# Half of the modulation weights in one transfer, freer PSUM banks and a new order in a transformer block with a gated spatial MLP

## The chip, the cores and the metric
One core of one Trainium2 chip runs the whole program. The metric is device microseconds (us) of one execution. Engines are called by their names and by the letters of the profile: TensorE is PE (its weight loads PEld), VectorE is DVE, ScalarE is ACT, GpSimd is POOL, SyncE is SP. SP and ACT issue the DMA transfers of this kernel.

## What is computed
An adaptive-layer-norm block on 2048 tokens of width 448, all tensors bf16. A vector `c` of 448 numbers gives six modulation vectors; then sliding-window attention (16 heads of 28, window 256), then a gated MLP whose gate mixes tokens with a 2048 x 2048 matrix:

```python
mod = (silu(c) @ w_mod).reshape(1, 6, 1, 448)      # w_mod: 448 x 2688
sa, ca, ga, sb, cb, gb = mod
h = layernorm(x) * (1 + ca) + sa
x = x + ga * attention(h, wqkv, wo)                 # 0 <= q - k < 256
h = layernorm(x) * (1 + cb) + sb
z = gelu(h @ w_in)                                  # 448 -> 1792
z1, z2 = z[:, :896], layernorm(z[:, 896:])
x = x + gb * ((z1 * (w_sp @ z2 + b_sp)) @ w_out)    # w_sp: 2048 x 2048
```

## The kernel before
**Tiles.** The 2048 tokens are 16 tiles of 128. The first half of the block runs over six blocks of tiles (1, 1, 2, 4, 4, 4). The width of 448 is cut into four chunks of 128 rows that start at rows 0, 128, 192 and 320 (`CH`); chunks 1 and 2 overlap in rows 192 to 255, and one of the two overlapping halves is zeroed or left out.

**Operations and their order.** The program is a list of some 1700 operations (`P.op`, with helpers `pe`, `dve`, `pool` and `load`), numbered in the order in which the code makes them. The string `ORDER` (line 177) lists these numbers in the order in which they are issued; `75/3` takes the fourth of the PSUM banks that the operation may use, `65.2` the third of its engine choices. `schedule` (line 81) reads the string and `emit` (line 115) turns it into one in-order stream for each engine, with a semaphore wait where an operation needs another engine's result, a DMA or a buffer that is still in use. An operation that waits holds up all that stands behind it on its engine; nothing else sets the order.

**Names used below.** `wmodA01`, `wmodA3`, `wmodAR0`, `wmodAR1`: loads of the part of w_mod for sa and ca (lines 496 to 499). `wqk03`, `wqkM`, `wqkR0`, `wqkR1`: loads of the query and key weights in raw form (lines 505 to 509). `x0`, `x0b`, `x1` to `x4`: tokens of tiles 0, 1, 2-3, 4-7, 8-11 and 12-15. `silu` (line 556): silu of c in column form, made from the row by `c_cols`. `modA` (line 585): 16 small matmul operations, eight for chunks 0 and 1 and eight (with an h) for chunks 3 and 2, all into one PSUM bank; `modAe` (line 588) evicts them to `modT`, the scale and shift. `l1_ts` (bn_stats, line 603), `ag`, `ve`, `rs`, `nm`: layer-norm statistics of tile t; `xn` the normalized tile (lines 624 and 625). `tr`: transposes of xn on TensorE for the first three blocks (line 674); `hT` evicts them with the modulation (lines 687 and 692). The last three blocks are transposed by DMA (`hx`, line 709) and modulated in place (`hm`, line 701). `wqkf` and `wqkr` spread the raw weights into padded form (lines 725 to 727). `qk<block>_<group>` are the query and key projections (lines 776 and following; for tile 0 partly from the raw weights, on 32 columns at a time), `qke` their evictions to `QKT` (lines 810 and 813), `v` and `ve` the values (lines 822 and 825).

**Attention.** For query tile j, `S<j>_<u>` writes scores of one key tile to two pairs of PSUM banks, `E<j>_<u>` takes the exponential on ScalarE (128 x 1024 elements, line 912, 90 of them, tiles `PT`), `M<j>_<u>` zeroes what the mask excludes on POOL (line 918), `PV` multiplies with the values, and `oq`, `rec`, `nrm`, `oT`, `wo`, `x1` normalize, transpose and project (lines 944 to 964). Projections of later blocks, and the first of the MLP, stand between the scores on TensorE. `gateB` (line 967) and four `woutg` multiplications (line 968) fold the last gate into w_out.

**The rest.** After the last scores come z2 and z1 of the MLP, the 448 matmuls with w_sp (`G`, whose stationary operand is z2), and the output projection, all on TensorE, with evictions on ScalarE and DVE.

The modulation's loads before, with the c row first on ScalarE's queue, are the lines that the diff below removes. The rows of chunk 2 that chunk 1 doesn't have (256 to 319) are loaded as two pieces of 64 rows, `wmodAR0` for sa into partitions 0 to 63 and `wmodAR1` for ca into partitions 64 to 127, and `c_cols` makes a fifth column of silu(c) so that each half of the chunk meets its own half of the column.

Of the kernel before, what the change touches and what calls it, by code (L numbers as in the profile page):

```python
# [181 lines left out]
142 155 14 252 156 248 157 20 159 160 161 188 189 499/0,0 162 163/0 164 165 501/4 166 168/1 173/2 174 167 21 250 249 254 143/3 251 144 175 16 169 170
171 176 145 146 147 113/0 114 115 116 117 191.1/4 196/0 253 148/3 149 255 256 172 150 151 152 337 190.1/2 195 333 257 258 262/3 177 261.1/1 500/1,1
504/0 192/3 193 194.1 22 197 11 178/1 179 180 181 182.1 123/4 124 516/0,1 125 126 127.1 520/2 228/0 229 230 231 232 15 497/3 208/0 209 210 211 331 18
19 498 218/2 219 517/6 212 266 220 221 222 523/1,0 526/8 223/1 259.1/0 224 198/2 199 225 502 200 524/10 201 202.1 226 505 506/0 503 507/0 203/3 204
205 206 265 260.1/2 207 508 338 335 233/2 234 235 236 237 332 227 521 537/0,1 541/7 518 213/3 334 214 519/0 509.1/1 336 339 263 215 216 217.1 340 525
522 527 528/0 243/1 244 245 246 264 267 270 268 269 341 345/3 538/8 238/3 239 240 544/1,0 344.1/4 420 241 539 418 247 271/1 326/0 327 281/2 282 548/6
328 349 329 330.1 272 273 283 545/1 551/1,0 343.1/0 284 285.1 342/2 242 552/5 306/3 307 308 309 291/0 310.1 274 554/4 292 293 294 419 348 565/0,1
566/10 347 529 530.1/0 549 276/3 277 275.1 278 311/2 312 313 314 279 569/0 570 295.1 510/0 416 417 315 286/0 287 572/0,1 573/9 288 289 531/1 301/1
576/3 302 303 304 280.1 579/0,2 580/2 290.1 540/0 582/8 546 547 555 550 542 543 553 305.1 421 296/1 297 298 299 593/1,0 556/0 557 532/0 533 567 534  # L190
535 577 300.1 511/1 512 513 514 594/1 600/2,1 414 536 597/4 574 575/0 568 571 346 351.1 558.1/1 583 353.1 578 581 598 559/2 350.1 515 560/1 561 562
352.1 604/7 607/1,0 584/0 563 564 601/6 602 585 932 379/0 415 380 381 382 383.1 929 364/1 365 931 610/10 595 621/2,0 964 605 366 367 586.1/1 368.1
608/9 384/0 385 930 386 387 422 388.1 587/2 934 622/2 623 625/3 628/1,2 632/5 369/1 370 371 372 373.1 606/0 629/7 603 423 424 428.1/1 611 596 426.1/2
609 599 635/0,2 612/0 636/9 588/1 589 590 591 592 432 359/0 360 649/0,1 427.1/3 638/6 653/4 321/1 322 966 323 324 613 361 362 656/1,2 650/1 935 325.1
399/1 400 401 402 425.1/0 633 363.1 967 946/0 947 948 949 660/10 614.1/1 950 962 951 952 953 663/2,0 626 403.1 316/1 317 318 319 657/0 661 630 954
637/0 627 639 624 960 615/1 664/8 677/2,1 654 320.1 634 631 666/9 640/0 641 651 354/1 355 356 357 358.1 658 659/0 652 642.1/1 431 965 961 963 968 969
678/5 667 684/0,2 681/7 688/6 685/1 689 643/2 655 662 665 668/0 682 374/1 375 376 377 378.1 691/1,2 694/9 669 644/0 645 646 1419 647 648 430 692/0 429
433.1 389/1 390 391 392 937 705/2,0 709/10 404/0 405 406 970 407 706/3 393.1 409/1 410 411 679 712/1,0 412 686 985 436.1 408.1 616/0 617 618 413.1
435.1 619 933 434.1 716/4 457/1 458 670.1/0 620 717 719/0,2 973/1 459 460 461.1 695/0 683 713/8 971/2 722/2 710 707 693 687 690 680 1421 733/1,2 936
696/0 697 720/9 734/7 737/1 394/1 395 396 938 397 398.1 452/0 453 454 455 740/1,0 467/1 735 671/2 468 469 470 456.1 672/0 673 674 675 983 744/6  # L200
747/0,2 471.1 447/1 698.1/1 448 449 941 738 676 739/0 714 972 987 450 451.1 741/0 742 699/1 750/5 761/1,2 736 751 743 745 748/1 762/7 746 765/6 749
752/0 975/0 437/1 438 439 440 441.1 768/1,0 772/5 942 977/2 974 753 754/1 763 715/0 708 711 769/10 770 700/1 701 702 703 704 775/0,2 984 978 755/0 721
718 723 773 724/0 725 462/1 463 464 465 776/1 778/3 466.1 789/0,1 793/4 989 442/0 976 726.1/0 443 444 940 445 990 446.1 790/2 482/1 483 484 485
796/2,1 797/8 771/0 486.1 727/1 766 981.1 777 774 779 764 767 988 780/0 800/0 979.1 487/1 939 803/2,0 986 806/7 945 991 804/3 488 489 490 472/0 473
474 475 980 817/1,0 821/9 801 491.1 756/1 781 757 758 759 992 476.1 782.1/1 728/0 729 791 730 731 818/5 798 760 824/0,2 828/6 783/0 784/1 785 786 819
825/1 732 1006 802/0 787 799 788 1423 822 1008 794 993 831/2,1 829 477/1 834/0 832/10 478 479 826 792 1010 480 845/0,1 998/1 795 846/4 481.1 807 805
808/0 955/1 809 849/8 1420 943 944 957 810.1/0 852/0,2 853/3 999 827/0 833 823 835 820 830 836/0 859/1,0 956 982.1 1075/0 1077 847 1076 856/10 1059/2
1000/0 1060 811/2 958 860/9 812/3 813 814 815 959 857 1422 1061 816 1012 862/2 873/1,0 874/5 1080/1 1079 1078 850 1081 1065/3 1082 877/6 1063 1062
1064 1067.1 1007 1013 854 855/0 848 996/2 1066 1009 880/0,1 837 851 997 994.1/1 838/0 863 1083 1011 1014 1015 884/3 885 1091/3 1092 1097/2 881/7 1096
839/0 1095 1001 1093 1094 1098.1 1099 861 858 864/0 865 887/1,0 888/0 1016 1107/1 1108 1109 492/3 493 494 495 890/1 1112/2 1111 866/0 1023/0 496 1110  # L210
867/1 901/0,1 902/9 1113 1115 868/0 1021/2 1114 869 870 871 908/0,2 872 905/10 882 1031 840/1 841 842 843 909/4 995 1004.1 1002.1 1302/7 1303 1304
1311/2 1314/6 1312 1313 912/8 915/2,0 1424 1317 1316 913 878 1003 1315 916/2 1005 844 1338/3 1339 1340 1167/2 1173 1169 1029 1030 875 1172 1168
1017.1/1 1171 1022 1170 1318 876/0 889 891 879 883 886 903 1319 1306/6 1307 1019/2 1305 1174/3 1123/3 1125 1126/2 1032 1127 892/0 893 917/0 1128 914
910 911 904 894.1/0 1176 1308 1129 1033 906 895/0 1124 918/7 919 907 1139/0 1429 1142 1141 1024 1143 1131 1342/0 1343 1144 1310 1341 1140 1329/6 1331
# [987 lines left out]
```

## Time and profile before
| | us |
|---|---|
| median of 3 runs | 271.27 |
| lowest, highest | 271.03, 271.34 |
| the profiled execution | 271.53 |
| its span, first to last instruction | 269.8 |

| engine | busy us | share of the span |
|---|---|---|
| PE | 258.7 | 96% |
| DVE | 168.2 | 62% |
| ACT | 133.2 | 49% |
| POOL | 104.1 | 39% |

The profile's page gives each engine's busy time, a picture of the span in 40 slices, the DMA queues, the chain of work that ended last (followed back from the last instruction to what released it) and groups of instructions. Its views can be narrowed to a stretch of the span; all times in them are us from the span's start. "Idle before" with a name behind an arrow says how long the engine sat before an instruction, and what ended that. A matmul's end is modelled, and matmuls overlap, so busy times of PE are an upper figure. The granted clock is the share of TensorE's full clock that was given.

### The profile page before, as it was taken

Reading aid. Unit: us, or ns where it says so; the run is one execution under the profiler, and the core shown is the slowest. Engines: PE = TensorE matmul, PEld = TensorE weight load, DVE = VectorE, ACT = ScalarE, POOL = GpSimd, SP = SyncE. Lnnn points to the kernel's source line nnn. Section 1 sums busy time; section 2 is a strip of 40 time slices with the busy share of each in tenths; the row PEclk is TensorE's granted clock in tenths of the full one; section 3 lists DMA queues with packets and bytes.
Section 4 is the critical chain, followed back from the end, with each engine's and each line's share of the span. In section 5 each row is a group of like instructions: output and inputs, shape, how many; then the busy total and the mean of one; then the engine's idle time right before and its main releaser. Section 6 shows DMA issues by size and latency. Waiting matters only on the chain.

```text
span 269.8 us, 7133 instructions
## 1 busy us (share of the span) xinstructions
PE 258.7 (96%) x3067; PEld 128.4 (48%) x3090; DVE 168.2 (62%) x390; ACT 133.2 (49%) x183; POOL 104.1 (39%) x162
## 2 busy tenths in 40 slices
PE   6799999999999799999999999999999999999995
PEld 2567444564545444544444444444444444444453
DVE  4499888887898899579968920731511534335343
ACT  4599899999999989986786200000000000100000
POOL 3566489889968848771732120000000000000000
PEclk9799999999999999999999999999999999999999
DMA  6945262298359434679599890000000000000103
GB/s 221 348 149 84 23 146 88 52 153 164 73 80 231 44 71 81 117 90 158 126 205 161 184 185 1 2 0 0 0 2 0 17 0 17 2 16 18 53 34 119
DMA packets 61052, 23.72 MB, mean 88 GB/s; under 512 B 49886, under 2 KB 60893, under 8 KB 61021
## 3 DMA queue, kind: packets, MB, share of 16 engines
q1 hardware_dynamic: 60715, 22.92, 42.2%
q8 instruction: 24, 0.39, 0.6%
q10 hardware_dynamic: 306, 0.35, 0.4%
q14 instruction: 7, 0.06, 0.1%
HBM read 9.36 MB, written 1.84 MB: 41 GB/s over the span
## 4 chain that ended last, share of the span: by engine, by line
PE 78%; ACT 8%; DVE 5%; DMA 4%; POOL 2%; issue 1%; ACTq 1%; SPq 0%; DVEq 0%
PE ps L457 73%; ACT PT L912 8%; PE ps L454 5%; DMA wmod_sb<-in_w_mod_dram 2%; DMA hT<-xn 1%; DVE st_all L603 1%; DVE w_out_sb L968 1%; POOL xn L624 1%; POOL PT L918 1%; DVE QKT L813 1%; PE ps L776 1%; DVE hT L701 1%; POOL rs_all L611 0%; DVE xn L625 0%; DVE hT L692 0%
## 5 line engine op out<-in xcount | busy, mean ns | idle before, releaser
L912 ACT ACTIVATE PT<-ps 128x1024 bf16<-128x1024 f32 x90 | 84.7, 1054 | 3.0 <-PE ps L457 2.5
L1041 ACT ACTIVATE z1T<-ps 128x512 bf16<-128x512 f32 x28 | 15.0, 602 | 82.5 <-PE ps L457 82.4
L1110 DVE TENSOR_TENSOR tmpg<-ps,bsp_bc 128x512 bf16<-128x512 f32 x28 | 19.1, 689 | 56.1 <-PE ps L457 55.7
L457 PE MATMUL ps<-QKT,z 128*128 128x512 bf16 x220 | 50.7, 379 | 0.2
L918 POOL TENSOR_SCALAR_AFFINE_SELECT PT<-PT 128x512 f32<-128x512 f32 x60 | 36.6, 635 | 4.8 <-ACT PT L912 4.6
L457 PEld LDWEIGHTS ps<-QKT,z 128*128 128x128 bf16 x224 | 21.9, 98 | 26.2 <-ACT z1T L1041 0.3
L611 POOL TENSOR_TENSOR rs_all<-ve_all,neghalf 128x1 f32<-128x1 f32 (+2 forms) x27 | 18.5, 686 | 32.6 <-DVE ve_all L610 32.2
L457 PE MATMUL ps<-w_spD,z 128*128 128x512 bf16 x109 | 26.0, 379 | 0.2
L457 PE MATMUL ps<-w_spC,z 128*128 128x512 bf16 x108 | 25.1, 379 | 0.2
L457 PE MATMUL ps<-hT,w_in_sb 128*128 128x512 bf16 (+1 forms) x95 | 23.5, 380 | 0.3 <-issue 0.2
L457 PE MATMUL ps<-w_in_sb,hT 128*128 128x448 bf16 (+1 forms) x102 | 22.8, 353 | 0.3 <-POOL PT L918 0.3
L457 PE MATMUL ps<-w_out_sb,z1T 128*128 128x448 bf16 (+2 forms) x119 | 22.8, 341 | 0.0
L457 PE MATMUL ps<-hT,WQK 128*128 128x512 bf16 (+2 forms) x118 | 20.7, 304 | 1.1 <-ACT QKT L810 0.4
L624 POOL TENSOR_SCALAR xn<-x_sb,rs_all,nm_all 128x512 bf16<-128x512 bf16 x25 | 19.7, 793 | 4.5 <-DVE nm_all L641 3.9
L603 DVE BATCH_NORM_STATS2 st_all<-z2raw 128x6 f32<-128x448 bf16 x32 | 18.8, 609 | 1.5 <-ACT z2raw L1018 1.0
L457 PE MATMUL ps<-QKT 28*128 28x128 bf16 x720 | 18.3, 217 | 1.5 <-ACT PT L912 1.1
L603 DVE BATCH_NORM_STATS2 st_all<-x_sb 128x6 f32<-128x448 bf16 x32 | 19.4, 616 | 0.3
L1132 DVE TENSOR_TENSOR fin<-ps,x_sb 128x448 bf16<-128x448 f32 (+2 forms) x17 | 9.9, 595 | 13.8 <-PE ps L457 13.7
L813 DVE CAST QKT<-ps 128x512 bf16<-128x512 f32 (+1 forms) x26 | 16.9, 655 | 2.1 <-PE ps L454 1.0
L457 PEld LDWEIGHTS ps<-QKT 28*128 28x128 bf16 x720 | 10.4, 92 | 16.4 <-ACT PT L912 13.4
L457 PEld LDWEIGHTS ps<-w_spD,z 128*128 128x128 bf16 x112 | 11.0, 98 | 13.0
L457 PEld LDWEIGHTS ps<-w_spC,z 128*128 128x128 bf16 x112 | 10.9, 98 | 13.1
(94 smaller groups left out, 325.9 us busy)
## 6 DMA issues: line engine op xcount, KB each, us to landing
wmod_sb<-in_w_mod_dram SPq DMA_DIRECT2D x8, 224.0 KB, 5.5
w_in_sb<-in_B_w_in_dram SPq DMA_DIRECT2D x8, 224.0 KB, 3.9
out_dram<-fin SPq DMA_DIRECT2D x16, 112.0 KB, 1.7
x_sb<-in_A_x_dram SPq DMA_DIRECT2D x3, 448.0 KB, 6.1
bsp_bc<-in_B_b_sp_dram SPq DMA_DIRECT2D x1, 512.0 KB, 5.3
wqk_raw<-in_A_wqkv_dram SPq DMA_DIRECT2D x1, 452.0 KB, 5.7
wmod_sb<-in_w_mod_dram SPq DMA_DIRECT2D x1, 448.0 KB, 4.7
wv_sb<-in_A_wqkv_dram SPq DMA_DIRECT2D x2, 224.0 KB, 5.9
```

The costliest lines, as they stand in the source:

```text
L454: last = e.matmul(out_[32 * j:32 * j + 32], lhsT=lhsT[:, 32 * j:32 * j + 32], rhs=rhs, start=st, stop=sp, tile_position=(0, 32 * j), **kw)
L457: return e.matmul(out_, lhsT=lhsT, rhs=rhs, start=st, stop=sp, **kw)
L603: st = [dve("%sst%d" % (name, i), prio, dve_ns(D), lambda e, i=i, s_=s_: e.bn_stats(st_all[:, slot, t, i, :], s_()), deps, tens) for i, s_ ...
L611: r = pool(name + "rs", prio, 420 + 148 * n, lambda e: e.tensor_tensor(rs_all[:, slot, t0:t1], ve_all[:, slot, t0:t1], neghalf[:, t0:t1], ...
L624: return e.tensor_scalar(dst, src, rs_all[:, slot, t:t + 1], nm_all[:, slot, t:t + 1], ALU.mult, ALU.add)
L701: return e.tensor_scalar(hT[:, c_, cols], hT[:, c_, cols], modT[:, base_col + 4 + c_:base_col + 5 + c_], modT[:, base_col + c_:base_col + ...
L813: return e.tensor_copy(QKT[:, g, cols], ps[:, ten.slot, 0:w])
L912: e_op = P.op("E%d_%d" % (j, ui), pr, [("act", 925, lambda e, e_in=e_in, e_out=e_out: e.activation(e_out(), e_in(), ACT.Exp, scale=SCALE)) ...
L918: ready = pool("M%d_%d" % (j, ui), pr - 50, pool_ns(512), lambda e, pt=pt, pat=pat, cm=cm, cmp=cmp: e.affine_select(out=pt32(pt.slot), in_ ...
L1041: g = P.op("z1g%d_%d" % (tb, ft), pr - 19, [("act", act_ns(512), lambda e: e.activation(z1T[:, ft, tb * 512:(tb + 1) * 512], ps[:, ten.slo ...
L1110: a = dve("ga%d_%d" % (tb, ft), pr, dve_ns(512), lambda e, tb=tb, ten=ten, tg=tg: e.tensor_tensor(tmpg[:, tg.slot, :], ps[:, ten.slot, :], ...
L1132: fs.append(dve("fin%s%d" % (nm, t), pr, dve_ns(c1 - c0), lambda e, t=t, ten=ten, ft_=ft_, c0=c0, c1=c1: e.tensor_tensor(fin[:, ft_.slot, ...
```

## The change
**Loads.** `wmodA3`, `wmodAR0` and `wmodAR1` (224, 56 and 56 KB) go; `wmodA23` comes, rows 192 to 447 in one transfer of 448 KB, on ScalarE's queue behind the c row as `wmodA3` was. Rows 192 to 255 are then in SBUF twice; the column of silu(c) for chunk 2 has zeros there. So `c_cols` has four matmuls and not five, one of the three copies of the c row on DVE goes (`cz2`), and `silu` works on four columns.

**Banks.** The single PSUM banks of `c_cols`, of `modA` and of the transposes of tile 1 (block 1) could be one of four, and can now be any of the eight.

```diff
-             load("wmodA3", -98, lambda e: e.dma_start(wmod_sb[:, 3, 0:2 * D], w_mod[320:448, 0:2 * D]), 128 * 2 * D * 2, order=[t_c], eng="act")]
-    t_wmAR = [load("wmodAR%d" % v, -98, lambda e, v=v: e.dma_start(wmod_sb[64 * v:64 * v + 64, 2, 0:D], w_mod[256:320, v * D:(v + 1) * D]), 64 * D * 2, eng="act")
-              for v in range(2)]
...
+             load("wmodA23", -98, lambda e: e.dma_start(wmod_sb[:, 2:4, 0:2 * D], w_mod[192:448, 0:2 * D].rearrange("(c p) n -> p c n", p=128)),
+                  256 * 2 * D * 2, order=[t_c], eng="act")]
...
-    tc_ten = Ten(B_D)
+    tc_ten = Ten(B_ALL)
...
-        for k, a in enumerate((0, 128, 256, 448, 320)):
-            last = mm(e, ps[:, tc_ten.slot, k:k + 1], crz[0:1, a:a + 128], one[0:1, 0:1], True, True)
+        for k in range(4):
+            last = mm(e, ps[:, tc_ten.slot, k:k + 1], crz[0:1, 128 * k:128 * k + 128], one[0:1, 0:1], True, True)
...
-            dve("cz1", -62, 180, lambda e: e.tensor_copy(crz[0:1, 320:384], crow[0:1, 256:320]), [t_c]),
-            dve("cz2", -62, 180, lambda e: e.tensor_copy(crz[0:1, 448:576], crow[0:1, 320:448]), [t_c])]
+            dve("cz1", -62, 180, lambda e: e.tensor_copy(crz[0:1, 320:512], crow[0:1, 256:448]), [t_c])]
...
-    mA_ten = Ten(B_D, guard=True)
+    mA_ten = Ten(B_ALL, guard=True)
...
-                for kc, sc in (((0, 0), (1, 1)), ((3, 3), (2, 4 if i == 0 else 2)))[h]:
-                    a = CH[mc] + (0 if kc == 2 else i * D)
+                for kc, sc in (((0, 0), (1, 1)), ((3, 3), (2, 2)))[h]:
+                    a = CH[mc] + i * D
...
-            ten = Ten(B_ALL if b == 0 else B_D, guard=True)
+            ten = Ten(B_ALL if b < 2 else B_D, guard=True)
```

**Order.** `ORDER` is new from end to end. Read with the names, each engine's stream changes most up to the first exponentials:

```
SP before    x0 wmodA01 wqk03 x0b wqkR0 wqkR1 x1 wqkM wv1 x2 woq2 x3 wmodG1 x4 wv0 ...
SP after     x0 wmodA01 wqk03 x0b wqkR0 x1 wqkR1 wqkM wv1 x2 wv0 wmodG0 wmodG1 woq2 x3 ...
ACT before   c wmodA3 wmodAR0 wmodAR1 silu0 silu exp0 hT0_3 wqkf1_3 hT0_0 wqkr0_k hT0_1
             wqkr0_q wqkf1_M qke0_5 wqkr1_q qke0_0 qke0_1 qke0_4 hT1_1 (6 qke) E0_0
             (6 qke) E0_1 hT2_1 E1_1 qke2_3 E1_0 (2 qke2) E1_3 E1_2 (3 qke2) E2_1 E2_0
             ve3 E2_3 E2_2 ve2 E2_4 E2_5 E3_0 E3_1 ve4 E3_2 ...
ACT after    c wmodA23 silu0 silu exp0 wqkf0_3 wqkr1_k wqkr0_k hT0_3 hT0_1 hT0_2 wqkf0_0
             qke0_1 qke0_5 qke0_4 qke0_0 hT1_1 qke0_6 wqkr1_q qke0_7 qke1_4 E0_0
             (7 qke) E0_1 qke1_7 hT2_1 ve0 E1_0 E1_1 (3 qke2) E1_3 E1_2 (2 qke2) E2_0 E2_1
             ve2 E2_2 E2_3 qke3_1 E2_4 E2_5 E3_1 E3_0 qke3_4 E3_2 ...
DVE before   ... xn0 zwq1 modAe hT0_2 l1_1st l1_1ag l1_1ve l1_2st l1_2ag l1_1nm wqkr1_k ...
DVE after    ... xn0 zwq0 l1_1st modAe l1_1ag l1_1ve wqkr0_q hT0_0 l1_1nm l1_2st l1_3st ...
POOL before  ... l1_4rs xn6 xn4 M0_0 M0_1 xn5 M1_1 M1_0 ...
POOL after   ... l1_4rs xn5 xn6 M1_0 xn4 M0_1 opad M0_0 M1_1 ...
PE before    ... modA (8) modA h (8) tr0_2 tr0_3 (6 warm) tr0_0 (4 warm) tr0_1 (3 warm)
             (tile 0: groups 0 5 1 4, one warm among them, then 2 with tr1, 6, 7)
             (tile 1: groups 2 5 0) S0_0 ...
PE after     ... tr0_1 warm modA (6) (6 warm) modA (2) modA h (8) tr0_3 (4 warm) tr0_2 tr0_0
             (3 warm) (tile 0: groups 5 4 1 0) tr1 (groups 7 6 2) (tile 1: group 4) S0_0 ...
```

After S1 the streams are alike up to small exchanges. On TensorE the operations between two scores are the same but for one or two. On DVE before: `oq11 rec11 woutg1 oq12 woutg0 oT11 woutg2 woutg3`; after: `oq11 rec11 woutg0 oq12 oT11 woutg3 woutg2 woutg1`. The masks, the exponentials, the MLP and the output have the same work as before.

More of the change, by code (lines that the diff above doesn't have):

```diff
@@ L182 @@
[L182 to L185, printed above, removed]
@@ L237 @@
+1674 1675/0 1619/2 1620 1495/4 1496 1564 1506 1609/2 1610 1667/7 1668 1621/4 1622 1549/0 1550 1497/1 1676 1611/7 1612 1498 1613/1 1614 1672 1551/4
+1553/3 1554 1555/7 1556 1677/5 1552 1678 1679/3 1680/2 1681 1682 1683
 """
@@ L395, in bass_adaLN_cond__sliding_block__mixer_gmlp__prompt_kernel @@
     one, _, e_ = alloc("one", [128, 16], BF16, at=e_ + 2 * D)
-    crz, _, _ = alloc("crz", [128, 576], BF16, at=e_)
+    crz, _, _ = alloc("crz", [128, 512], BF16, at=e_)
     ps = nc.alloc_psum_tensor("ps", [128, 8, 512], F32)
```

124 lines of the change are left out of this document (62 added, 62 removed).

## The prediction
> **What bounds the kernel now.** I read the stretches of the span first (columns: stretch, its length, then busy us and instruction count of PE, PEld, DVE, ACT, POOL, granted clock, DMA share, GB/s).
> ```profile
> 36.00:96.00 60.00, 57.80 (x1397) 30.70 (x1402) 51.56 (x107) 59.58 (x65) 54.07 (x79) 1.00 0.60 114
> 104.00:267.00 163.00, 161.98 (x996) 75.36 (x1009) 81.56 (x187) 38.69 (x54) 26.40 (x41) 1.00 0.34 62
> ```
> From 104 on TensorE is busy 161.98 of 163.00 us, so the end comes when TensorE has done what is left. From 36 to 96 ScalarE is busy 59.58 of 60.00: the exponentials (tiles PT, line 912) pace TensorE there. A microsecond won before 36 therefore arrives at the end whole, if ScalarE stays fed; won anywhere else on the other engines it is worth nothing. Next the chain that ended last (start, us, what), in its early part:
> ```profile
> 1.36 0.37 ACTq L498
> ...
> 2.32 5.93 DMA wmod_sb<-in_w_mod_dram
> ...
> 8.38 3.06 PE ps L457 x33
> 11.44 0.65 PE ps L776 x20
> ...
> 12.42 1.10 PE ps L776 x42
> ...
> 13.84 0.73 DVE hT L692 x2
> ...
> 23.58 0.53 SPq L709
> ...
> 24.15 4.03 DMA hT<-xn
> ...
> 28.26 1.38 DVE hT L701 x4
> ```
> Two waits stand in it. The last modulation rows land at 2.32 + 5.93 = 8.25. The DMA transposes of tokens 4 to 7 land at 28.18, and only then are they modulated (hm3, line 701). What both do to ScalarE is in its timeline (start, us, line, operation, idle before it):
> ```profile
> 10.44 0.41 ACT L726 ACTIVATE WQK<-wqk_raw 64x256 bf16<-64x256 bf16 x1
> 10.84 0.46 ACT L687 ACTIVATE hT<-ps,modT 128x128 bf16<-128x128 f32 x1
> 14.40 0.81 ACT L687 ACTIVATE hT<-ps,modT 128x128 bf16<-128x128 f32 x2
> 15.10 1.21 ACT L810 ACTIVATE QKT<-ps 128x128 bf16<-128x128 f32 x6
> 16.21 1.02 ACT L912 ACTIVATE PT<-ps 128x1024 bf16<-128x1024 f32 x1
> ...
> 21.24 0.38 ACT L810 ACTIVATE QKT<-ps 128x256 bf16<-128x256 f32 x1
> 21.50 1.03 ACT L912 ACTIVATE PT<-ps 128x1024 bf16<-128x1024 f32 x1
> ...
> 31.34 1.94 ACT L912 ACTIVATE PT<-ps 128x1024 bf16<-128x1024 f32 x2 [0.64 <-PE ps L457]
> 33.94 1.02 ACT L912 ACTIVATE PT<-ps 128x1024 bf16<-128x1024 f32 x1 [0.66 <-PE ps L457]
> ```
> The first exponential (E0_0) starts at 16.21. ScalarE then idles 0.64 and 0.66 before E2_4 and E3_0, behind the projections that waited for the transposes. From there it is full.
>
> **The change part by part.** The sum is made on the profiled execution, 271.53 us (span 269.8 and 1.73 around it); the median of the runs shown is 271.27, so I subtract from that.
>
> *The loads.* First KB and us to landing of the transfer that grows, then first and last issue and us to landing of the two key and query pieces of 56.5 KB (R0, R1) and of token tile 1 (x0b), and a stretch:
> ```profile
> wmod_sb<-in_w_mod_dram ACTq DMA_DIRECT2D x1, 224.0 KB, 4.4
> L508 SPq DMA_DIRECT2D wqk_raw<-in_A_wqkv_dram x2: 669/693/717, 2.7 to 3.4; - x2
> DMA to landing us min/median/max: 5.4/5.6/5.9
> L488 SPq DMA_DIRECT2D x_sb<-in_A_x_dram x1: 468/468/468, 2.2 to 2.2; - x1
> DMA to landing us min/median/max: 6.2/6.2/6.2
> 5.00:6.00 1.00, 0.76 (x2) 0.00 (x0) 0.68 (x2) 1.00 (x1) 0.02 (x1) 1.00 1.04 398
> ```
> Removed: three transfers on ScalarE's queue (224 + 56 + 56 KB). Added: one of 448 KB, so 112 KB more. It is issued where the 224 KB one was (1.36; that landed at 5.8). Its other 224 KB share 398 GB/s with SP's queue; at half of that they take 1.15 us, so it lands near 6.9 (bounds: 5.8, as the 224 KB alone; 8.25, as the rows it replaces). The 112 KB push SP's loads back by 0 to 0.3 us (112 KB at 398 GB/s is 0.29): x0b from 8.4 to 8.4–8.7, R0 (2.7 + 5.9) from 8.6 to 8.6–8.9. R1 (3.4 + 5.4) now stands behind a 224 KB token load, another 0.6: from 8.8 to 9.5–9.7.
>
> The Trainium skill, "DMA: Bandwidth & Descriptors", section "Issuing engines are not separate DMA queues", speaks against the change: a transfer started from ScalarE runs on the same 16 engines as SP's and interleaves with them. By it the whole 0.29 us falls on SP's loads; without it, nothing, and the sum below would move by no more than that. The 1.04 mean DMA share in the last row fits it.
>
> *The modulation (modAe).* Now 8.96; its DVE row, and the statistics of tile 1 that stood behind it:
> ```profile
> 8.96 0.17 DVE L588 TENSOR_TENSOR modT<-ps,zero_one 128x8 f32<-128x8 f32 x1 [3.11 <-PE ps L457]
> 9.56 0.62 DVE L603 BATCH_NORM_STATS2 st_all<-x_sb 128x6 f32<-128x448 bf16 x1
> ```
> In the new order these statistics stand ahead of modAe, and they need x0b: 8.4–8.7 + 0.62 = 9.0–9.3. So the earlier landing is worth nothing here: modAe comes at about 9.3, 0.3 later than before. I cost the merged transfer at nothing; its cover is x0b, and it would count only past 8.7.
>
> *Tile 0 to queries and keys.* Before, ScalarE and DVE mix hT0 with weight copies, and the last hT0 ends at 10.84 + 0.46 = 11.30. After, ScalarE does two 0.41 copies first (from 8.9: 9.7), then three hT0 in a row (0.81 for two: 1.2): 10.9. DVE does 0.18 + 0.15, a copy of 0.21 that waits for R1 (9.9), and hT0_0: 10.3. TensorE starts at 10.4 on what is ready. Its 62 matmuls took 0.65 + 1.10 with 0.33 between (12.42 - 12.09); 64 without that gap take 1.8: 12.2, against 13.5. Tile 1's transposes (0.4) follow; its statistics and normalization are ready by 11.6. ScalarE has four evictions of 0.2 to 0.28 to do by then and starts hT1_1 at about 12.9, before 14.40. Then 0.81, three evictions (1.21 for six: 0.6) and a copy (0.41): E0_0 at 14.7, **1.5 us earlier** (bounds: 0.6, if every landing is at its late end and the copies chain up; 1.8, if all are at the early end).
>
> *From E0_0 to E3_0.* ScalarE gets two more 128-column evictions (0.4), one fewer of 256 (0.38) and one of 512 columns, whose nearest row is the 512-column activation:
> ```profile
> L1041 ACT ACTIVATE z1T<-ps 128x512 bf16<-128x512 f32 x28 | 15.0, 602 | 82.5 <-PE ps L457 82.4
> ```
> 0.4 - 0.38 + 0.60 = +0.6, which the idle 1.3 can take. A second 512-column eviction after E3_0 replaces a V eviction of about the same size: 0. On POOL the last normalization before the transposes (xn4) moves behind one mask, not two, but this is tile 1's (M1_0), which needs E1_0:
> ```profile
> 20.41 1.22 POOL L918 TENSOR_SCALAR_AFFINE_SELECT PT<-PT 128x512 f32<-128x512 f32 x2
> 21.63 0.76 POOL L624 TENSOR_SCALAR xn<-x_sb,rs_all,nm_all 128x512 bf16<-128x512 bf16 x1
> L709 SPq DMA_TRANSPOSE hT<-xn x4: 1255/1287/2277, 19.2 to 24.2; - x4
> DMA to landing us min/median/max: 2.6/3.9/4.4
> ```
> E1_0 is now the first of tile 1, behind one V eviction (0.55): 0.75 earlier than the first one was, it ends at 20.6. Mask to 21.2, xn4 to 22.0 (22.4 before), landing 2.6 to 4.4 later: 24.6 to 26.4, against 28.18. The longer issue (2277 against 1287) and that landing are accidents of this execution that I don't carry over. Then the transposes no longer end last: TensorE reaches these projections about 1.0 to 1.5 earlier by its own queue. I take E3_0 **1.2 us earlier** (between 0 and 1.6).
>
> *From E3_0 on.* TensorE's sequence has the same work between any two score blocks, within one operation, and ScalarE the same operations: 0, bounds -0.5 and +0.8 from reshuffled DVE and POOL work. One place differs on the chain:
> ```profile
> 93.51 1.05 DVE L968 TENSOR_TENSOR w_out_sb<-w_out_sb,ps 128x896 bf16<-128x896 bf16 x1
> 94.48 0.43 DVE L953 STREAM_TRANSPOSE oT<-o_sb 128x256 f32<-128x256 f32 x1
> 96.48 1.94 ACT L912 ACTIVATE PT<-ps 128x1024 bf16<-128x1024 f32 x2 [0.66 <-PE ps L457]
> ```
> oT11 stood behind two of the 1.05 multiplications, and TensorE's wo11, S14_0 and ScalarE's E14_0 behind oT11. Now one stands ahead, and oT11 comes right after the transpose before it. Of the 0.66 I take **0.4** (bounds 0 and 0.66). Sum: 1.2 + 0.4 = 1.6; 271.27 - 1.6 = **269.7 us**.
>
> **The rivals.** *The gain is hidden*: the transposes again land near 28.2. For it: two of four took long here. Against: 22.0 + 4.4 = 26.4. E3_0 gains nothing, and of the 0.4 half may go to the extra evictions: 271.1.
>
> *Slower, through the last transpose*: xn4 waits for E1_0, mask M1_0 and ScalarE's queue. If E1_0 ends no earlier than 22.53 (21.50 + 1.03, where it ended before) plus the V eviction put ahead (0.55), then 23.1 + 0.63 + 0.76 = 24.5, and at 4.4 to land 28.9: all that hangs on hm3 is 0.7 late, and the extra 0.6 on ScalarE has no idle to go into: 271.3 + 0.7 + 0.6 - 0.4 = 272.2. It decides from an xn4 that ends after 23.8.
>
> *Slower, through the clock*: granted clock by stretch, and the warm-up matmuls:
> ```profile
> 10.00:11.00 1.00, 1.00 (x7) 0.71 (x6) 0.93 (x4) 1.00 (x4) 0.34 (x1) 0.50 1.10 367
> 13.00:14.00 1.00, 1.00 (x36) 0.80 (x28) 0.16 (x1) 0.93 (x4) 0.39 (x1) 0.91 1.09 377
> 3.01 2.74 PE L457 MATMUL ps<-warm 128*128 128x512 bf16 x6
> 170.46 10.74 PE ps L457 x49
> ```
> At half clock a 512-column matmul takes about 0.45 (2.74 / 6), later 0.22 (10.74 / 49). Here the half clock ended by 13. The new order leaves TensorE waiting near 9 to 10.4; if the clock stays half until about 16, some 45 matmuls of 128 columns cost 0.055 more each (a quarter of 0.22), 2.3 us with the first V projections: 269.7 + 2.3 = 272.0. Against it: TensorE still has some 2.6 us of work between 9.5 and 12.9. The Trainium skill, "TensorE: Matmul & The Clock Gate", Part 1, has such a rule: the clock follows the activity of free-running windows of about 3.4 us. The half-clock stretch here is about that long.
>
> *It doesn't do what it says*: the merged rows land no earlier than 8.25. Then the modulation is ready near 9.1, still covered by x0b's 9.3: the same 269.7.
>
> **How the numbers follow.** Forecast 0.62, hidden 0.13, last transpose 0.15, clock 0.10. I count 0.2% (0.54 us) as what a measurement of this kernel can tell from no change. So faster 0.62, same 0.13, slower 0.25. The forecast's own range is 268.7 (1.6 + 0.66 + a little) to 270.7. The range goes to 272.5, past the centres of both slower cases, and down to 268.6.
>
> **What would show it.** Right: the modulation's first half-matmuls wait for wmod_sb until about 7, modAe near 9.3, hT1_1 (line 687, two at once) near 12.9, E0_0 near 14.7, no idle on ScalarE over 0.3 before E2_4 and E3_0, E14_0 without its 0.66. Wrong: E0_0 after 15.7 (landings or copies chain up); E0_0 early but hm3 at 28 or later (last transpose); a granted clock of 0.50 past 13; or ScalarE busy under 59 of the 60 us after E3_0, which would be new waits in the reshuffled part that I cost at nothing.

## The result, and where the profile after differs

The kernel after takes 269.75 us (median of 9 runs, 268.79 to 270.98), the kernel before 271.27 in the same session: ratio 0.9939, 95% interval 0.9912 to 0.9967. That is 1.5 us faster, inside the range and 0.05 from the forecast. The profiled execution of after took 268.95 (span 267.2), so it is one of the faster ones; the profiled pair differs by 2.6, the medians by 1.5. One profile below (before_stats) is of an execution of 302 us, at a granted clock of 0.85 or less from 5 us on; only VectorE's and GpSimd's order in its first 20 us is read.

ScalarE's timeline of after, for the rows that the prediction showed of before (start, us, line, operation, idle before it):
```profile
8.71 1.13 ACT L683 ACTIVATE hT<-ps,modT 128x128 bf16<-128x128 f32 x3
11.31 0.82 ACT L683 ACTIVATE hT<-ps,modT 128x128 bf16<-128x128 f32 x2
13.17 1.03 ACT L908 ACTIVATE PT<-ps 128x1024 bf16<-128x1024 f32 x1
...
28.32 0.60 ACT L806 ACTIVATE QKT<-ps 128x512 bf16<-128x512 f32 x1 [0.32 <-PE ps L454]
29.03 1.94 ACT L908 ACTIVATE PT<-ps 128x1024 bf16<-128x1024 f32 x2
31.63 1.94 ACT L908 ACTIVATE PT<-ps 128x1024 bf16<-128x1024 f32 x2 [0.66 <-PE ps L457]
```
The line numbers are four lower than before (908 was 912). E0_0 starts at 13.17, 3.04 earlier than 16.21. The exponential with 0.66 idle ahead of it, the last in before's list (called E3 below), stood at 33.94 and stands at 31.63: 2.31 earlier. So 0.7 of the early start is lost between 13 and 32.

VectorE's timeline of after names the place where it is lost:
```profile
8.31 0.15 DVE L584 TENSOR_TENSOR modT<-ps,zero_one 128x8 f32<-128x8 f32 x1
...
11.21 0.73 DVE L688 TENSOR_SCALAR hT<-ps,modT 128x128 bf16<-128x128 f32 x2 [0.15 <-PE ps L457]
...
15.21 0.17 DVE L606 TENSOR_SCALAR ve_all<-mv_all 128x4 f32<-128x4 f32 x1
...
25.94 1.38 DVE L697 TENSOR_SCALAR hT<-hT,modT 128x512 bf16<-128x512 bf16 x4 [0.58 <-DMA hT<-xn]
```
hm3 (line 697) still waits for a DMA transpose, 0.58 us (0.75 before). The chain that ended last in after, as the view follows it back (start, us, what), runs through the same transposes, but starts at another load:
```profile
4.12 4.90 DMA wqk_raw<-in_A_wqkv_dram
...
9.77 0.86 PE ps L772 x48
...
18.10 0.92 ACT PT L908
...
19.09 0.64 POOL PT L914
19.73 0.76 POOL xn L620
...
21.81 4.11 DMA hT<-xn
...
25.94 0.42 DVE hT L697
```
The modulation rows are gone from it; the first piece is R1 (wqkR1), landed at 9.02. The view leads over the exponential E1_0, its mask and xn4 to the last transpose, but these did not hold it up: xn4 ended at 19.73 + 0.76 = 20.49, and the last issue began at 21.81, 0.05 behind the end of the third (19.80, 1.96 long). In all the profiles of the table below but that of tr_early the four issues follow each other like that, 0.04 to 0.05 apart.

The first 48 matmuls of line 772 take 0.86 in this chain. All 64 of tile 0 are done at 10.84, 1.07 after the first start; these are the first and the last row of them on TensorE:
```profile
9.77 0.57 PE L772 MATMUL ps<-hT,wqk_raw 128*32 128x128 bf16 x28 [0.69 <-DVE hT L688]
...
10.61 0.23 PE L772 MATMUL ps<-hT,WQK 128*32 128x128 bf16 x4
```
In before 62 of them took 0.65 + 1.10.

Two stretches of after: first the one in which TensorE stood idle in before (its 7.00:8.00 had a PE share of 0.00), then one in which before ran at half clock:
```profile
7.00:8.00 1.00, 1.00 (x28) 0.95 (x26) 0.23 (x1) 0.62 (x1) 0.59 (x2) 1.00 1.11 342
...
10.00:11.00 1.00, 1.00 (x66) 0.89 (x52) 1.00 (x4) 0.71 (x3) 1.00 (x2) 1.00 1.10 382
```
In after TensorE is busy from 7 to 8 (warm-up matmuls stand between the two halves of the modulation) and the granted clock stays at 1.00.

The loads of after (KB and us to landing), the first weights and the merged transfer:
```profile
wqk_raw<-in_A_wqkv_dram SPq DMA_DIRECT2D x1, 452.0 KB, 5.6
...
wmod_sb<-in_w_mod_dram ACTq DMA_DIRECT2D x1, 448.0 KB, 4.8
```
and its token tile 1, by line (first and last issue, then us to landing):
```profile
L488 SPq DMA_DIRECT2D x_sb<-in_A_x_dram x1: 467/467/467, 2.2 to 2.2; - x1
...
DMA to landing us min/median/max: 5.5/5.5/5.5
```
The merged rows land at 1.34 + 4.8 = 6.1 (8.25 before), token tile 1 at 2.2 + 5.5 = 7.7 (8.4 before).

**All profiles side by side.** Each column is one number of the profile: mean ns of the 48 query and key matmuls of tile 0 that read the raw weights (line 776 of before, 772 of after); start of hT1_0 on VectorE, of the first DMA transpose, of hm3 (L701/697) and of the E3 exponential with the 0.66 idle; last, the span from that exponential to the end. before_stats is left out for the reason above.

| kernel | median us | ratio to before, interval | qk ns | hT1_0 | transpose | hm3 | E3 | E3 to end |
|---|---|---|---|---|---|---|---|---|
| before | 271.27 | | 299 | 13.84 | 19.18 | 28.26 | 33.94 | 235.9 |
| after | 269.75 | 0.9939 (0.9912–0.9967) | 220 | 11.21 | 17.15 | 25.94 | 31.63 | 235.6 |
| after_again | 269.76 | 0.9940 (0.9917–0.9963) | 220 | 11.27 | 17.99 | 26.17 | 31.86 | 236.0 |
| loads_only | 269.34 | 0.9915 (0.9891–0.9940) | 222 | 11.19 | 16.53 | 26.03 | 32.20 | 235.8 |
| order_only | 269.58 | 0.9935 (0.9912–0.9957) | 220 | 11.68 | 17.62 | 26.58 | 32.27 | 236.1 |
| no_warm | 271.23 | 0.9991 (0.9972–1.0010) | 312 | 13.13 | 19.29 | 27.41 | 33.39 | 235.8 |
| before_warm | 270.37 | 0.9963 (0.9946–0.9979) | 221 | 12.60 | 17.94 | 27.10 | 32.78 | 235.8 |
| loads_nowarm | 269.13 | 0.9920 (0.9898–0.9942) | 309 | 11.35 | 16.68 | 25.75 | 31.92 | 235.5 |
| after_st7 | 269.57 | 0.9933 (0.9912–0.9955) | 220 | 11.20 | 16.79 | 26.14 | 31.83 | 235.5 |
| tr_early | 269.06 | 0.9916 (0.9897–0.9935) | 220 | 11.50 | 15.14 | 25.40 | 31.40 | 235.8 |
| loads_wv | 269.35 | 0.9909 (0.9885–0.9932) | 222 | 11.18 | 16.52 | 25.11 | 31.38 | 235.5 |
| loads_wv_zv | 269.17 | 0.9908 (0.9885–0.9930) | 222 | 12.69 | 17.99 | 25.81 | 31.99 | 235.5 |
| after_split | 270.09 | 0.9947 (0.9927–0.9967) | 220 | 12.66 | 18.82 | 27.71 | 33.40 | 235.8 |

Three things stand in it. From E3 to the end every kernel takes 235.5 to 236.1, old order or new: **everything that the change brings, it brings before 34 us**. And in the order of before, the first transpose starts 5.33 to 5.34 after hT1_0 in all five kernels that keep that part of it (before, before_warm, loads_only, loads_nowarm, loads_wv): VectorE's statistics of tiles 4 to 7, one power on GpSimd and one normalization stand between, and they move as one block. In the new order the distance is not fixed (5.6 to 6.7, without tr_early).

The third is what stands before E3. In seven kernels (before, after, after_again, order_only, before_warm, after_st7, after_split) hm3 waits 0.58 to 1.03 for a transpose, and E3 starts 5.68 or 5.69 behind hm3. In the other six hm3 waits for no transpose, E3 starts 5.98 to 6.27 behind it, and the chain that ended last runs over TensorE's queue there. So the transposes are the limit in seven of the thirteen, and not in all.

A profile is one execution, though. Under the same loads the whole stream of loads lands up to 1.0 us earlier or later (token tile 1 at 7.7 in after, at 8.7 in no_warm), and the runs of after spread over 2.2 us. Rows of single profiles show what waits for what; sizes are taken from the medians, and kernels that ran beside another before are compared by their ratios.

### The profile page after: what moved, and what is told of

It reads as the page before. It is cut to its first block, busy times and chain, and to the rows that moved or that the text cites. A ratio compares the mean times of both kernels' runs of the same rounds, so it can differ in the third digit from the quotient of the medians.

```text
span 267.2 us, 7093 instructions
## 1 busy us (share of the span) xinstructions
PE 258.8 (97%) x3059; PEld 127.8 (48%) x3059; DVE 166.0 (62%) x389; ACT 133.2 (50%) x182; POOL 103.8 (39%) x163
## 4 chain that ended last, share of the span: by engine, by line
PE 76%; ACT 14%; DMA 3%; DVE 3%; SPq 1%; POOL 1%; issue 1%
PE ps L457 71%; ACT PT L908 12%; PE ps L454 5%; DMA wqk_raw<-in_A_wqkv_dram 2%; DMA hT<-xn 2%; ACT QKT L806 1%; DVE w_out_sb L964 1%; POOL PT L914 1%; ACT hT L683 1%; SPq L488 1%; DVE oq L940 1%; DVE oT L949 0%; PE ps L772 0%; POOL xn L620 0%; SPq L505 0%
## 5 line engine op out<-in xcount | busy, mean ns | idle before, releaser
L457 PE MATMUL ps<-QKT,z 128*128 128x512 bf16 x224 | 50.0, 379 | 0.0
L457 PEld LDWEIGHTS ps<-QKT,z 128*128 128x128 bf16 x224 | 21.9, 98 | 26.4 <-ACT z2raw L1018 0.2
L457 PE MATMUL ps<-w_spC,z 128*128 128x512 bf16 x112 | 25.8, 379 | 0.0
L457 PE MATMUL ps<-hT,w_in_sb 128*128 128x512 bf16 (+1 forms) x101 | 25.2, 380 | 0.0
L457 PE MATMUL ps<-w_in_sb,hT 128*128 128x448 bf16 (+1 forms) x110 | 24.4, 353 | 0.4 <-DVE oq L940 0.2
L457 PE MATMUL ps<-w_out_sb,z1T 128*128 128x448 bf16 (+2 forms) x119 | 21.9, 341 | 0.0
L457 PEld LDWEIGHTS ps<-QKT 28*128 28x128 bf16 x720 | 10.4, 92 | 15.6 <-ACT PT L908 11.3
L809 DVE CAST QKT<-ps 128x512 bf16<-128x512 f32 (+2 forms) x26 | 16.1, 624 | 2.8 <-PE ps L457 1.8
L457 PEld LDWEIGHTS ps<-w_out_sb,z1T 128*128 128x128 bf16 x119 | 11.6, 98 | 9.9
```

Of the source, the lines that this page charges most:

```text
L457: return e.matmul(out_, lhsT=lhsT, rhs=rhs, start=st, stop=sp, **kw)
L809: return e.tensor_copy(QKT[:, g, cols], ps[:, ten.slot, 0:w])
```

## The experiments

The first four kernels were to tell three theories apart. **O**: the new order brings the gain, and the merged transfer is covered, as predicted. **L**: the merged transfer brings it. **C**: the gain is TensorE's half-clock stretch, which is gone.

**after_again.** The kernel after, unchanged, on the chip of the next three.

> The changed kernel once more, as the control of this set: 269.7 us, 0.5 or so either way, first exponential (E0_0) near 13.2. Theory O (the new order of the prologue makes the gain, the merged transfer is covered) and theory L (the merged transfer makes it) say nothing different here. Theory C (the gain is the half-clock stretch of TensorE at 9.5 to 12.9, which is missing in the changed kernel's profile) expects that a run with such a stretch is about 1 us slower than one without.

269.76, ratio 0.9940: the result stands.

**loads_only.** The order and the banks of before; the loads and the four columns of after.
```diff
 ORDER of before, without wmodAR0 wmodAR1 cz2
-wmodA3 wmodAR0 wmodAR1   # 224 + 56 + 56 KB
+wmodA23                  # 448 KB
```


> The order of before with the merged transfer and four columns of silu(c), banks as before. O: modAe is earlier, but the hT0 evictions still alternate with the weight copies, so E0_0 stays within 0.4 of 16.2 and the time is 271.0 to 271.5. L: modAe goes from 9.0 to about 7.5, E0_0 to about 15, time 269.7 to 270.3. C: the half clock stays, time as before.

269.34, ratio 0.9915: the merged transfer alone brings all of the gain. Its modulation, in the timeline of VectorE, does not wait for token tile 1 as in after, because in the order of before it stands ahead of that tile's statistics:
```profile
6.91 0.17 DVE L584 TENSOR_TENSOR modT<-ps,zero_one 128x8 f32<-128x8 f32 x1 [1.14 <-PE ps L457]
```
6.91 against 8.96: two microseconds that the prediction had put at nothing. O, which needed the order for the gain, falls.

**order_only.** The reverse: the order and banks of after with the three transfers of before.
```diff
 ORDER of after, with wmodAR0 wmodAR1 behind wmodA3 and cz2 behind cz1
-wmodA23
+wmodA3 wmodAR0 wmodAR1
```


> The new order and banks with the three old transfers and five columns. O: modAe at 9.0 to 9.3, E0_0 13.6 to 14.2, time 269.7 to 270.3. L: the small rows land after 8 and SP's loads are as late as before (tile 1's tokens at 8.4), E0_0 at 14.5 to 15.5, time 270.5 to 271.3.

269.58, ratio 0.9935: the order alone brings all of it too. Each half is worth the whole, so the halves do not add up, and there must be something that both of them do. The modulation comes at 9.01 here, no earlier than before, and still hT1_0 comes 2.2 earlier (11.68). Both kernels run the query and key matmuls at 220 to 222 ns, before at 299. That spoke for C.

**no_warm.** The kernel after without its warm-up matmuls from the tenth on.
```diff
-    for i in range(22):
+    for i in range(9):
```


> The changed kernel without its last 13 warm-up matmuls (they compute nothing that is used). O and L: nothing waits for them, 269.7 and E0_0 at 13.2. C: the clock is 0.50 from about 9.5 to 12.9, E0_0 at 14.2 to 14.7, and the time 0.7 to 1.3 higher.

271.23, ratio 0.9991. TensorE waits 1.59 for the modulation and the granted clock falls (stretch, length, then PE, PEld, DVE, ACT, POOL, granted clock):
```profile
9.00:10.00 1.00, 0.29 (x1) 0.10 (x1) 0.87 (x5) 1.00 (x4) 0.77 (x3) 0.75 1.09 367
...
15.00:16.00 1.00, 0.97 (x13) 0.91 (x10) 0.38 (x4) 1.00 (x3) 0.78 (x2) 0.50 1.07 206
```
From 9.5 to 16.3 it stays at a half. Thirteen matmuls whose results nobody reads are worth the whole change. Part of the late rows of this profile belongs to its loads (token tile 1 landed 1.0 later than in after); the median of its 12 runs does not rest on them. And what is lost here is lost on TensorE itself: hm3 (27.41) waits for no transpose, and the chain that ended last stays on TensorE from 10.65 to past 30.

**before_warm.** If C is all, warm-ups in the hole of before should do what the change does. Loads and order of before:
```diff
 modA1_3
+warm22 ... warm35        # 14 matmuls of 256 columns
 modA0_0h
```


> The kernel before with its own loads, order and banks, and 14 more warm-up matmuls of 256 columns between the two halves of the modulation, where TensorE waited 1.77 us for the last rows. Theory C (the half-clock stretch of TensorE from 9.5 to 12.9 us is what both the loads alone and the order alone take away): the granted clock is 1.00 throughout, the modulation still comes near 9.0, the query and key matmuls run at about 0.055 us per group of four, the first exponential comes near 14.7 (16.21 before), and the time is 269.6 to 270.3. Theories L and O (the earlier landing, or the new order of hT0 and the copies, is what counts): no change, 271.2 to 271.5, clock or not.

270.37, ratio 0.9963. The hole is filled (TensorE's timeline):
```profile
6.09 1.69 PE L457 MATMUL ps<-warm 128*128 128x256 bf16 x14
8.02 0.54 PE L457 MATMUL ps<-sc_sb,wmod_sb 128*128 128x1 bf16 x16 [0.24 <-DMA wmod_sb<-in_w_mod_dram]
```
and the query and key matmuls are fast (group by shape: count, busy us, mean ns):
```profile
L776 PE MATMUL ps<-hT,wqk_raw 128*32 128x128 bf16 x48 | 1.4, 221 | 0.0
```
hT1_0, hm3 and E3 all come 1.16 to 1.24 earlier; the median gains 0.9 to 1.0 (ratio 0.9963), just less than expected. The half clock is thus worth about 1.0 of the 1.7 to 1.9 that after_again and order_only gain against the 271.50 of before beside them.

**loads_nowarm.** The loads alone, without warm-ups: does the earlier landing need the full clock?
```diff
 ORDER of loads_only
-warm8 ... warm21
```


> The merged transfer in the order of before, without the warm-up matmuls from the ninth on (14 of them). Theory C: TensorE waits over 1.5 us between 7 and 9, the clock falls to 0.50 from about 9 on, the first exponential comes at 14.5 or later (13.40 with the warm-ups) and 1.2 to 2 us of the time are lost against the loads alone, 270.6 to 271.4. Theory L (the earlier landing brings the gain by itself): the time stays within 0.4 of the loads alone, 269.0 to 269.8.

269.13, ratio 0.9920: nothing is lost, so the earlier rows bring the gain in this order without the full rate, and C falls as the one cause. The matmuls are slow, as slow as under the granted 0.50 of no_warm (312 ns; group by shape):
```profile
L771 PE MATMUL ps<-hT,wqk_raw 128*32 128x128 bf16 x48 | 2.1, 309 | 0.8 <-ACT hT L682 0.6 <-DMA wqk_raw<-in_A_wqkv_dram 0.2
```
and the granted clock (third number from the end of a stretch's row) does not show it. The page of this profile has no row for the clock at all, where those of before and no_warm have one, so no record stands behind this 1.00:
```profile
10.00:12.00 2.00, 2.00 (x48) 1.78 (x37) 1.59 (x6) 1.93 (x8) 1.84 (x3) 1.00 1.10 359
```
E0_0 comes at 14.20, 0.8 later than in loads_only (13.40), and the time does not care. hT1_0 is at 11.35 all the same: with the rows two microseconds earlier, even slow matmuls are done when VectorE gets there. This suggested **theory D**: what counts is hT1_0, not E0_0. From hT1_0 the chain would go over VectorE's statistics of tiles 4 to 7 and four transposes, one after the other, to hm3 and E3. By D the earlier rows, the full rate and the new order are three ways of bringing hT1_0 forward.

The traces hold a simpler reason why nothing is lost here. TensorE's values for the first tiles need the first half of the V weights (`wv0`), and in loads_only TensorE had time to spare before they landed:
```profile
17.21 1.31 PE L457 MATMUL ps<-wv_sb,hT 128*128 128x448 bf16 x6 [1.23 <-DMA wv_sb<-in_A_wqkv_dram]
```
There TensorE's earlier work ended at 15.99. In loads_nowarm it ended at 16.79, and the weights land at 8.77 + 8.10 = 16.87:
```profile
16.92 1.31 PE L456 MATMUL ps<-wv_sb,hT 128*128 128x448 bf16 x6
```
In both kernels the chain that ended last runs from this landing over TensorE's queue. The 0.8 lost at half rate went into a wait that was there anyway, so this pair does not decide between E0_0 and hT1_0.

**after_st7.** VectorE takes the statistics of tile 7 ahead of qke1_0, for which it waited 0.41.
```diff
-qke1_0 ... l1_7st0
+l1_7st0 qke1_0
```


> The kernel after with one pair of DVE operations exchanged: the statistics of token tile 7 ahead of the eviction qke1_0, for which DVE waited 0.41 us. If the four serial DMA transposes still end last, so that their start sets E3_0: they start 0.3 to 0.4 earlier (16.75 in place of 17.15), and the time falls by 0.2 to 0.4, to about 269.4. If TensorE's queue has become the bound: no change, 269.75.

269.57 (ratio 0.9933) against 269.75 (0.9939): below what this can tell. The transposes start 0.36 earlier (16.79), as expected, and hm3 comes no earlier (26.14), since one of the four issues took 2.22 us in this execution (1.25 to 1.3 otherwise; in after 1.96). Such a long issue is in most of the profiles here and eats a small gain. Inconclusive.

**tr_early.** The fourth transpose reads an older tile, so that it is issued early.
```diff
-in_=xn[:, xn_ten[t].slot, :]))], [xn_op[t]], [xn_ten[t]], ...
+in_=xn[:, xn_ten[2 if t == 4 else t].slot, :]))], [xn_op[2 if t == 4 else t]], ...
```


> The kernel after with the fourth transpose (token tile 4) reading token tile 2 instead, so that it is issued first, near 14.8, and only three are left to issue from 17.15 on; this leaves out the right data of token tile 4. If the transposes end last: the modulation of tokens 4 to 7 (line 697) starts 1.0 to 1.5 earlier than 25.94, the idle of 0.58 before it goes, and the time falls by 0.4 to 1.3 until the next limit (TensorE's queue, or the last projections) takes over, 268.5 to 269.3. If TensorE's queue is the bound already: no change, 269.75.

269.06, ratio 0.9916. The wait of hm3 is gone:
```profile
24.87 0.61 DVE L821 CAST Vaug<-ps 128x448 bf16<-128x448 f32 x1
25.40 1.37 DVE L697 TENSOR_SCALAR hT<-hT,modT 128x512 bf16<-128x512 bf16 x4
```
hm3 follows the V eviction directly, 0.54 earlier than in after, but E3 only 0.23 earlier: TensorE's queue is the next limit. The median is 0.7 lower (0.5 below after_st7 on the same chip). The intervals overlap, so the size is open; that the transposes end last in after, and that the next limit is 0.23 behind them, the rows show.

**before_stats.** D by itself: before, with only the statistics of tiles 6 and 4 moved into VectorE's wait of 1.31.
```diff
-hT1_0 ... l1_6st0 ... l1_4st0
+l1_6st0 l1_4st0 hT1_0
```


> The kernel before with one move: DVE takes the statistics of token tiles 6 and 4 ahead of hT1_0, in the 1.31 us for which it waited there; loads, order of TensorE, banks and warm-ups as before. Theory D (the chain that counts runs from hT1_0 over DVE's statistics of tiles 4 to 7 and their normalization to the four serial DMA transposes and E3_0; the half clock only matters because it delays hT1_0): the half-clock stretch stays, the first exponential stays at 16.2, but the transposes start near 18.1 (19.18 before), the modulation of tokens 4 to 7 near 27.1, E3_0 near 32.8, and the time falls by 0.9 to 1.2, to 270.1 to 270.5. Rival (the half clock or the first exponential by itself sets the time): within 0.3 of before, 271.1 to 271.6.

271.43, ratio 0.9996 (0.9980 to 1.0013): no change. VectorE's timeline says why:
```profile
12.45 1.08 DVE L603 BATCH_NORM_STATS2 st_all<-x_sb 128x6 f32<-128x448 bf16 x2
13.99 0.73 DVE L692 TENSOR_SCALAR hT<-ps,modT 128x128 bf16<-128x128 f32 x2 [0.46 <-PE ps L457]
14.64 0.16 DVE L610 TENSOR_SCALAR ve_all<-mv_all 128x2 f32<-128x2 f32 x1
15.62 0.16 DVE L641 SCALAR_TENSOR_TENSOR nm_all<-mv_all,rs_all 128x2 f32<-128x2 f32 x1 [0.82 <-POOL rs_all L611]
```
The statistics fit into the wait, but they had been the cover of another: behind hT1_0 stands the variance of tiles 2 and 3, GpSimd's power on it ends at 15.58, and l1_2nm waits for that. With the two statistics gone from there, VectorE stands 0.82. The transposes start at 19.20 (19.18 before). That execution ran at another clock (its query and key matmuls took 227 ns, 299 in before), so the equal start of the transposes is a weak hint. The move did not shorten the chain, so it is no test of D. What fell is the expectation that work before hT1_0 is free.

**loads_wv.** In loads_only TensorE stands 1.23 for the first half of the V weights at 17.21; here they are loaded earlier.
```diff
-x2 woq2 x3 wmodG1 x4 wv0
+x2 wv0 woq2 x3 wmodG1 x4
```


> The loads alone (merged transfer, order of before) with the first half of the V weights moved forward on SP's queue, right behind token tiles 4 to 7, since in that kernel TensorE stood 1.23 us for it at 17.2. Theory D with that landing as the next limit: the wait goes, the transposes become the last to end again, E3_0 comes 0.5 to 1.0 earlier than with the loads alone (32.20 to about 31.5), and the time falls to 268.6 to 269.1 (269.34 with the loads alone). If the transposes or TensorE's queue were just behind: 269.2 to 269.5.

The wait goes (the load landed at 17.2 in loads_only, at 12.0 here), and E3 comes at 31.38, 0.82 earlier than in loads_only. That profiled execution took 268.63, but the median is 269.35, the same as loads_only. The six runs spread from 267.94 to 269.69. Not shown to be faster.

**loads_wv_zv.** The same, with the zero fill of the V weights on GpSimd and the statistics of tile 6 ahead of hT1_0.
```diff
-zv on DVE ... hT1_0 ... l1_6st0
+l1_6st0 hT1_0 ... zv on POOL behind l1_2rs
```


> As the kernel with the V weights moved forward, and DVE relieved on the chain of D: the zero fill of the V weights goes to POOL, and the statistics of tile 6 stand ahead of hT1_0. D: the transposes start 0.3 earlier (16.2 in place of 16.5), and the time falls by 0.2 to 0.3 more, 268.4 to 268.9. Rival (TensorE's queue is the next limit at an E3_0 of about 31.4, as with the early transpose): no further change.

269.17, ratio 0.9908, next to loads_wv: no difference. In its profile, whose loads came some 0.5 later than in loads_wv, the statistics of tile 6 waited for their tokens (landed at 12.13), hT1_0 moved back to 12.69 and the transposes to 17.99, the opposite of what was expected.

**after_split.** The merged transfer as two of 128 full rows.
```diff
-             load("wmodA23", ..., wmod_sb[:, 2:4, 0:2 * D], w_mod[192:448, ...] ...
+             load("wmodA2", ..., wmod_sb[:, 2, 0:2 * D], w_mod[192:320, 0:2 * D]), ...
+             load("wmodA3", ..., wmod_sb[:, 3, 0:2 * D], w_mod[320:448, 0:2 * D]), ...
```


> The kernel after with the merged transfer cut into two of 128 full rows (224 KB each) on the same queue. If it is the full rows that count, in place of the two 56 KB pieces that read half rows: landings as after (modulation near 8.3, token tile 1 near 7.8), 269.5 to 270.0. If it is the one transfer in place of several: the rows and token tile 1 land 0.4 to 0.7 later, the modulation comes near 8.8, and the time is 270.0 to 270.4.

270.09, ratio 0.9947 (0.9927 to 0.9967). The median lies in the second range, 0.09 above the first, and the interval holds after's 0.9939, so the time does not decide. The issues of the two transfers with their us to landing, and token tile 1:
```profile
L498 ACTq DMA_DIRECT2D wmod_sb<-in_w_mod_dram x1: 371/371/371, 1.3 to 1.3; - x1
...
DMA to landing us min/median/max: 5.0/5.0/5.0
...
L500 ACTq DMA_DIRECT2D wmod_sb<-in_w_mod_dram x1: 467/467/467, 1.7 to 1.7; - x1
...
DMA to landing us min/median/max: 6.9/6.9/6.9
...
L488 SPq DMA_DIRECT2D x_sb<-in_A_x_dram x1: 467/467/467, 2.2 to 2.2; - x1
...
DMA to landing us min/median/max: 7.1/7.1/7.1
```
The loads of this execution all came late (token tile 1 at 9.3), so only differences within it are read. The second transfer lands 2.3 after the first (8.6 against 6.3), as the pieces of before did (7.8 and 8.25 against 5.8). That points to the one transfer, and not to the full rows, as what brings the rows in early; it rests on one execution.

**Verdict.** Shown: the gain lies before E3 in every kernel; either half of the change brings it; full rate of TensorE without anything else brings 1.0; in the order of before the earlier rows bring it without full rate, while in the new order the gain is lost without full rate (no_warm). So there is more than one chain ahead of E3: it ends with the transposes in seven kernels, and with TensorE's queue in the other six. Not shown: D as the one account. The fixed 5.34 in five kernels and tr_early speak for it, loads_nowarm and no_warm, where the transposes do not end last, speak against it, and the kernel that was to test its middle part did not shorten the chain. The banks were changed with the order alone, never by themselves; what they bring is not known. No kernel is shown to beat after: the lowest that computes everything (loads_nowarm, 269.13) overlaps with it in the intervals.

## Why the prediction was right, and which steps were not

The number was right, within 0.05, and that is in part luck: E0_0 came twice as far forward as forecast, the term behind E3 did not come, the transposes stayed last where they were to be overtaken, and the transfer costed at nothing is worth the whole gain in the old order. One rival was real.

*The merged transfer at nothing, behind the cover of x0b.* The cover was named rightly for the new order: modAe comes right behind the statistics of tile 1, and order_only (269.58) and after_again (269.76) do not differ. But it is a cover that the new order itself puts up. In the old order the rows are worth the whole gain. The step asked what the transfer adds to the order and not what each part brings by itself.

*SP's loads pushed back by 0 to 0.3.* In the pair they came earlier, not later. The weights that stand ahead of token tile 1 on SP's queue, in before:
```profile
wqk_raw<-in_A_wqkv_dram SPq DMA_DIRECT2D x1, 452.0 KB, 5.7
```
Token tile 1 landed 1.0 behind them in before (8.4 against 1.7 + 5.7 = 7.4), and 0.4 behind them in after (7.7 against 1.7 + 5.6). With modAe behind that tile it came at 8.31, not 9.3, and R1 landed at 9.0, not 9.5. The Trainium skill, "DMA: Bandwidth & Descriptors", section "Issuing engines are not separate DMA queues", from which the prediction took that the 112 KB more fall on SP's loads, speaks of shared engines and not of the number of transfers. No run here shows the delay: over all the profiles token tile 1 lands at 7.7 to 8.7 with the merged transfer and at 8.0 to 8.5 with the three (after_split aside), so the 0.29 is lost in the spread, and so is the sign. What does stand clear of it is the landing of the rows: 6.1 to 7.0 in nine profiles with the merged transfer, 7.9 to 8.3 in the four with three transfers.

*Tile 0's matmuls, E0_0 1.5 earlier.* It was 3.04. The mis-sized term is "Its 62 matmuls took 0.65 + 1.10 ...; 64 take 1.8": those rows were taken at half clock and carried over as they stood, where the 64 take 1.07 in after at full clock. That is 0.7 of the 1.5 that E0_0 came earlier than forecast; another 0.6 is their start, 9.77 in place of 10.4, behind the earlier modulation, and the rest lies between them and hT1_1 (11.31 in place of 12.9). The prediction quoted the half-clock row and used it only for the rival that made the time worse. That the change could remove the stretch was not asked.

*E0_0 to E3: 1.2 earlier, and the transposes no longer last.* xn4 ended at 20.5, not 22.0, and the transposes landed at 25.9, inside the forecast 24.6 to 26.4. But TensorE was ready earlier too, so the transposes were last all the same (0.58 idle ahead of hm3, the idle of 0.66 ahead of E3 unchanged), and E3 came 2.31 earlier in the pair. The sign "no idle over 0.3" was wrong. So was the reading behind it, that the 0.66 ahead of E3 comes from the transposes: it stands there in all thirteen kernels, also in the six in which hm3 waits for none. What sets it is open.

*oT11: 0.4.* E14_0's wait went from 0.66 to 0.51 in the pair:
```profile
93.96 1.94 ACT L908 ACTIVATE PT<-ps 128x1024 bf16<-128x1024 f32 x2 [0.51 <-PE ps L457]
```
and the pair's spans from E3 on differ by 0.3, but over all kernels those in the new order take no less from E3 to the end (235.5 to 236.1) than those in the old (235.5 to 235.9). The term is not seen.

*From E3 on: 0.* Right: 235.5 to 236.1 throughout.

*The sum.* 2.3 at E3 in the profiled pair, with an after that is 0.8 below its own median; 1.5 in the medians. The forecast 1.2 + 0.4 had the right size by luck, through a term too small before E3 and one behind it that the runs do not show.

*The rivals.* The one through the clock has its mechanism in no_warm: waits of TensorE near 8 to 9.5, half clock to 16.3, and 271.23 where the rival gave 272.0: the half clock cost 1.5 against after_again, where the rival had 2.3 (its own 45 x 0.055 is already 2.5). After escapes it because warm-ups stand where before stood still. The hidden gain (271.1) and the late transpose (272.2) did not come: xn4 ended 3.3 ahead of the 23.8 from which the latter decides. The rows landed at 6.1, so the rival in which they come no earlier fell too.

## What to carry to other kernels

Before a duration is carried from one profile to another, look at the clock of the stretch that it comes from, and ask whether the change moves the idle time that caused it; here that missed 0.7, and the clock stood in a quoted row. Where a change has two parts, cost each against the old kernel alone: two parts that relieve the same chain don't add up, and a cover found in the new order may be built by the new order. An idle slot on an engine is not free for work that had been covering a later wait. And when a slower kernel loses nothing, look for a wait that took up the loss before concluding that the slow part does not count.

## What the runs showed of the hardware

- A listed clock of 1.00 can stand for no record. In loads_nowarm the matmuls took 309 ns (312 at a granted 0.50 in no_warm, 220 at full rate) beside a listed 1.00, in a profile whose page has no row for the clock. The rate has to be read from the durations of one shape. The Trainium skill, "TensorE: Matmul & The Clock Gate", Part 1, says that the trace's events of the gate have been seen to be unreliable and are not to be trusted fully; this trace agrees. Of the 54 executions of before beside the experiments, 25 list a mean clock of 0.999 or 1.000 and have a median of 271.8, the 29 with 0.992 to 0.994 one of 271.2: a clean clock went with a longer time. No profile of the former was taken, so their matmul durations, and whether their clock was recorded, are not known.
- A second transfer on ScalarE's queue, issued 0.4 us after the first, landed 2.0 to 2.3 us after it, with 56 KB (before) and with 224 KB (after_split), one execution each; one transfer of 448 KB landed at 6.1, no later than 0.4 behind the first 224 KB of before.
- The stream of loads at the start lands up to 1.0 us earlier or later from one execution to the next under the same loads, and the spread of the times (2.2 us in after) is of that order.
